# Transposed chunks laid out in runs of 384 columns, and the whole order of a fused recurrence and convolution laid anew

## The chip, the cores and the metric

The kernel runs on one core of a Trainium2 chip. The metric is the device time of one execution in microseconds (us). The compute engines of the core are PE (matrix products and transposes), DVE, ACT and POOL (elementwise work); SP issues the transfers, and 16 transfer engines carry them out. Each engine works through its own queue in order and waits on semaphores for the others.

## The reference

```python
def _attn_ref(r, k, v, w, u):          # B, H, S, D = 4, 8, 768, 48
    state = np.zeros((B, H, D, D))
    for t in range(S):
        cur = np.einsum('bhd,bhe->bhde', u[None] * kt, vt)
        y[:, :, t] = np.einsum('bhd,bhde->bhe', rt, state + cur)
        state = wt[:, :, :, None] * state + np.einsum('bhd,bhe->bhde', kt, vt)

def _moe_ref(x, w_proj, filter_fft, w_out):   # x: the y above as 4 x 768 x 384
    x1, x2, x3 = split(x @ w_proj, 3)
    x2_conv = irfft(rfft(x2, axis=1) * rfft(filter_fft, axis=0), axis=1)
    return ((x1 * x2_conv * x3) @ w_out).astype(np.float32)
```

A linear recurrence with a decay w and a bonus u gives y for 4 batches, 8 heads, 768 steps and 48 channels. Then y, as 768 x 384 for each batch, is projected three ways; the second projection is convolved along time with a filter, multiplied by the other two and projected out. Inputs and output are float32.

## The kernel before

Time is cut into chunks of 128 steps: 24 chunks, six to a batch (c is the chunk of all, ci its place in the batch). For each chunk the four slices of w, k, r and v are loaded (ldw, ldk, ldr, ldv: 192 KB each, into rings of six buffers). ACT takes the logarithm of w (lw); PE sums it along time by triangular masks (cs, ce) and ACT takes exponentials (en or enp, eq). These scale k and r (kh, q), which PE transposes (tqk) and ACT or DVE copies out of the bank (tT). sc is the product of the two within the chunk, mt its masked copy, kv and S the state that is handed on. rk, rku and cc make the bonus (r times k times u, summed over a head) and vc is v times it. y is summed in a bank; a step yb starts with a matmul that adds vc, a step y leaves it out, and DVE's xn adds it while it copies the bank (after yb, ACT's xc copies it). yt transposes y in three blocks of 128 channels, and xT copies that to SBUF.

In place of a transform of 768 points the kernel folds time. For the chunks 3 to 5 of a batch, sa and sb add and subtract the transposed chunk and its counterpart of the first half (into sd), fp and fm fold the sums once more (into fo), and x2 projects these by the second slice of w_proj. f transforms them by a matrix, da, db, ua and ub multiply by the filter's transform, pp adds, and i1 and i2 transform back. p1 and p3 are the other two projections: PE multiplies a slice of w_proj (stationary) by 384 columns of the transposed y (moving), three matmuls for each step. yy multiplies by their product g, po projects out, o copies the result and st stores it.

The three slices of w_proj and w_out are loaded by ldp0 to ldp3 (576 KB each, into o0), and ACT casts them (wc).

The order of all this is written out by hand in a string, ORDER (line 37), of 1094 words. Each word holds an engine (S, P, A, V and G for SP, PE, ACT, DVE and POOL), an operation with its chunk or its batch and part, and behind @ a bank. Line 864 emits word after word, so each engine's queue is the words of its letter in their order. Waits come from the buffers that the words share, and a word with ! also waits for DVE's last operation of a certain kind.

Before the change the transposed y of a batch lies as three rows (blocks of channels) of 768 columns, and a chunk is a piece of 128 columns in each:

```python
    xT_b = ring("xT", 2, [L, CB, S], BF16)       # L = 128, CB = 3, S = 768
    sd_b = ring("sd", 2, [L, CB, HALF], BF16)    # HALF = 384
```

Of the kernel before, what the change touches and what calls it, by code (L numbers as in the profile page):

```python
# [38 lines left out]
V:ang2 V:ang0 V:mem0 V:angn V:mem4 P:cs2@0 V:mem6 P:ce2@1 S:ldfilt A:en2 P:zs29@2 A:lw0 P:ce1@2
G:uc! G:mkd! V:mem5 V:fs S:ldk1 A:sin S:ldr1 S:ldk0 S:ldv0 S:ldr0 P:z7@0 P:zs2@0 P:ce0@3 P:hf0@0  # L40
P:cs1@4 V:rsc P:zs2@5 P:cs0@5 A:eq1 A:en1 A:eq0 A:ht0.1 A:v0 P:hf1@2 V:fd S:ldr3 P:hf2@4 P:hf3@3
A:enp0 A:ht0.0 V:rk1 V:q1 V:mem2 V:hr0.1 A:ht1.1 G:kh1! V:khp0 V:hr0.0 P:kv0@5 S:ldk3 V:hr1.1 G:q0!
A:eqp2 P:tqk0@0 V:S0 P:hf4@5 A:ht1.0 G:rk0! S:ldw3 V:rku1 P:tqk1@4 S:ldk2 S:ldr2 A:he P:hf5@2 G:rk3!
A:lw3 A:ph2 V:tT0 P:ce3@0 V:cc1 S:ldv1 V:rku0 A:ht2.1 S:ldw4 A:tT1 V:hr1.0 V:cc0 P:cs3@3 P:sc0@8
G:kh2! V:hr2.1 G:vc0! P:mtr1@4 V:qp2 P:tqk2@1 G:rk2! A:enp3 A:ht2.0 A:ms1 V:mt0 A:v1 S:ldw5 S:ldv2
P:kv1@5 A:tT2 V:rku3 V:rku2 V:hr2.0 P:sc1@8 P:mtr0@1 P:yb0@2 S:ldr4 S:ldk4 A:lw4 A:eq3 G:hb2! V:khp3
P:ce4@0 A:lw5 A:hb0 V:S1 P:cs5@3 A:xc0 P:cs4@5 V:ms0 V:cc2 G:q3! P:tqk3@2 V:mt1 A:eq4 V:cc3 P:mtr2@0
P:sc2@8 G:vc1! V:mt2 A:v2 A:en5 A:tT3 V:mc0 S:ldk5 P:kv2@3 G:rk4! G:vc2! A:ms2 A:enp4 P:yb1@2
P:sc3@8 G:q4! V:khp4 A:mc1 V:mt3 P:ce5@1 P:y2@4 S:ldw6 S:ldv3 A:v3 A:xc1 A:mc2 S:ldr5 V:S2 P:yt0@5
P:tqk4@2 P:kv3@0 G:kh5! A:eq5 P:yt1@1 G:vc3! S:ldw7 S:ldv5 A:lw6 V:rk5 V:rku4 V:rku5 A:lw7 V:S3  # L50
A:tT4 S:ldv4 S:ldr6 A:xT0 V:cc4 P:ce6@3 S:ldk6 G:q5! P:sc4@8 P:tqk5@2 V:xn2 G:v4! P:cs6@4 V:mt4
V:xT1 P:yb3@5 A:eq6 P:cs7@3 P:kv4@0 A:tT5 G:vc4! A:v5 A:en6 S:ldw8 S:ldp1 P:sc5@8 A:xc3 G:q6! V:cc5
P:yb4@2 P:yt3@5 P:yt2@4 G:rk6! A:lw8 A:xc4 P:ce7@1 V:S4 A:xT2 V:mt5 A:eq7 V:sa3 V:sb3 A:xT3 G:vc5!
# [842 lines left out]
```

## Time and profile before

| | |
|---|---|
| median of 3 runs | 158.87 us (158.29 to 159.4) |
| the profiled execution | 159.96 us, its span 158.3 us |
| busy PE, DVE, ACT, POOL | 136.4, 134.1, 131.2, 107.5 us |
| moved by DMA | 27.59 MB in 105,844 packets |
| mean granted clock of PE | 0.987 of full speed |

The span is the time from the first to the last instruction; the execution's own time is a little longer. Busy time is summed over an engine's instructions; matmuls overlap, so PE's is not its work at full pace. A transfer is issued by SP and lands some microseconds later; at most eight are under way, since each issue waits for the one eight places ahead of it.

### The profile page before, as it was taken

To read this page: it belongs to the slowest core of one execution; us is meant where nothing else is said; L and a number is where in the kernel's file an instruction comes from. 1 tells how busy PE (TensorE), PEld (TensorE's weight loads), DVE (VectorE), ACT (ScalarE), POOL (GpSimd) and SP (SyncE) were. 2 spreads that over 40 slices of the span, in tenths; PEclk is the share of its full clock that TensorE was granted. 3 is DMA by queue.
4 is the path that set the end of the run, shared out by engine and by line. 5 is a ranking of instruction groups with operands and counts; after the bars stand their busy time and mean duration, and the time that the engine had idled before them with its cause. 6 is when DMAs were issued, how large, how long until landed. Compare 5 with 4: busy or idle time off the path is not lost.

```text
span 158.3 us, 4054 instructions
## 1 busy us (share of the span) xinstructions
PE 136.4 (86%) x1492; PEld 89.0 (56%) x1492; DVE 134.1 (85%) x271; ACT 131.2 (83%) x274; POOL 107.5 (68%) x130
## 2 busy tenths in 40 slices
...
PEclk9999999999789999999999999999999999999998
DMA  5999989989898999979999979999940020000856
GB/s 105 189 297 178 205 162 211 209 171 255 178 234 207 205 195 196 214 149 222 203 177 261 222 148 221 190 206 246 247 159 0 4 99 4 0 2 35 326 205 233
DMA packets 105844, 27.59 MB, mean 174 GB/s; under 512 B 100320, under 2 KB 105824, under 8 KB 105824
## 3 DMA queue, kind: packets, MB, share of 16 engines
...
q8 instruction: 11, 0.18, 0.5%
...
## 4 chain that ended last, share of the span: by engine, by line
PE 40%; ACT 14%; DMA 13%; DVE 13%; SPq 9%; issue 4%; POOL 4%; ACTq 0%; POOLq 0%; DVEq 0%
SPq L452 9%; PE p L669 8%; PE x L700 7%; PE po L796 5%; DMA o<-in_moe_w_proj_dram 4%; DMA ldw<-in_w_dram 4%; DMA ldr<-in_r_dram 3%; ACT qkT L233 3%; PE f L720 3%; PE tqk L542 3%; DMA ldv<-in_v_dram 2%; PE sc L555 2%; PE i L754 2%; PE f L715 2%; DVE UA L742 2%
## 5 line engine op out<-in xcount | busy, mean ns | idle before, releaser
L669 PE MATMUL p<-xT,wproj 128*128 128x384 bf16 x144 | 29.6, 326 | 0.9 <-ACT qkT L233 0.9
L523 POOL TENSOR_TENSOR rk<-ldr,ldk 128x384 bf16<-128x384 f32 x21 | 21.3, 1018 | 6.2 <-DMA ldr<-in_r_dram 2.0
L562 DVE TENSOR_TENSOR mt<-sc,mask_excl 128x1024 bf16<-128x1024 f32 x21 | 25.5, 1213 | 0.0
L233 ACT ACTIVATE qkT<-tqk 128x1024 bf16<-128x1024 bf16 x21 | 21.8, 1039 | 0.7 <-PE tqk L542 0.7
L520 POOL TENSOR_TENSOR qk<-ldr,eq 128x384 bf16<-128x384 f32 x20 | 20.1, 1004 | 2.9 <-ACT eq L487 1.1
L536 POOL TENSOR_TENSOR vc<-v,cc 128x384 bf16<-128x384 bf16 x24 | 19.9, 832 | 2.8 <-ACT ab L233 1.3
L516 POOL TENSOR_TENSOR qk<-ldk,en 128x384 bf16<-128x384 f32 x12 | 12.0, 1000 | 12.8 <-ACT E L422 7.4
L669 PEld LDWEIGHTS <-wproj 128*128 128x128 bf16 x144 | 12.7, 97 | 8.8 <-issue 1.4
L542 PE MATMUL tqk<-ident,qk 128*128 128x128 bf16 x192 | 14.8, 219 | 2.3 <-DVE qk L510 1.1
L458 ACT ACTIVATE lg<-ldw 128x384 bf16<-128x384 f32 x24 | 12.8, 540 | 4.3 <-DMA ldw<-in_w_dram 4.3
L542 PEld LDWEIGHTS <-qk 128*128 128x128 bf16 x192 | 12.1, 98 | 5.6 <-issue 2.7
L796 PE MATMUL po<-wout,y 128*128 128x384 bf16 x72 | 14.3, 326 | 0.3 <-DVE y L788 0.3
L754 PE MATMUL i<-m_b,P 128*128 128x384 bf16 x72 | 14.0, 325 | 0.0
L233 ACT ACTIVATE x<-p 128x384 bf16<-128x384 f32 x24 | 11.9, 510 | 1.8 <-PE p L669 1.7
L233 ACT ACTIVATE ab<-x 128x384 bf16<-128x384 f32 x24 | 11.6, 509 | 1.8 <-PE x L700 1.6
L529 DVE TENSOR_REDUCE cc<-rku 128x8 f32<-128x384 bf16 x24 | 13.0, 540 | 0.0
L233 ACT ACTIVATE xT<-yt 128x384 bf16<-128x384 bf16 x20 | 10.1, 513 | 2.7 <-DVE sd L646 2.3
L462 PE MATMUL cs<-lg,mask_incl 128*128 128x384 bf16 x24 | 7.6, 331 | 5.5 <-ACT lg L458 5.1
L745 DVE TENSOR_TENSOR UB<-f,T 128x768 bf16<-128x768 f32 x11 | 10.3, 949 | 2.0 <-PE f L720 2.0
L487 ACT ACTIVATE eq<-ce 128x392 f32<-128x392 f32 (+1 forms) x23 | 11.6, 507 | 0.2
L591 DVE TENSOR_TENSOR S<-kv,eq 128x384 bf16<-128x384 f32 x20 | 10.9, 547 | 0.5 <-PE kv L583 0.5
L233 ACT ACTIVATE v<-ldv 128x384 bf16<-128x384 f32 x19 | 10.4, 545 | 1.2 <-DMA ldv<-in_v_dram 1.2
(143 smaller groups left out, 372.1 us busy)
## 6 DMA issues: line engine op xcount, KB each, us to landing
ldw<-in_w_dram SPq DMA_DIRECT2D x24, 192.0 KB, 3.9
ldk<-in_k_dram SPq DMA_DIRECT2D x24, 192.0 KB, 3.8
ldr<-in_r_dram SPq DMA_DIRECT2D x24, 192.0 KB, 4.0
ldv<-in_v_dram SPq DMA_DIRECT2D x24, 192.0 KB, 3.8
out_dram<-o SPq DMA_DIRECT2D x12, 192.0 KB, 2.5
out_dram<-filt SPq DMA_DIRECT2D x12, 192.0 KB, 2.1
o<-in_moe_w_proj_dram SPq DMA_DIRECT2D x3, 576.0 KB, 5.9
...
```

The costliest lines, as they stand in the source:

```text
L233: return nc.scalar.activation(out=o, in_=i, func=AF.Copy)
L452: nc.sync.dma_start(out=ld[x][c % LD], in_=src[b, :, ci * L:ci * L + L, :].rearrange("h t d -> t h d"),)
L458: nc.scalar.activation(out=lg_b[c % 3][:, :, 0:D], in_=ld["w"][c % LD], func=AF.Ln)
L520: return two(e).tensor_mul(qk_b[c % 3][:, 0, :, 0:D], ld["r"][c % LD], eq)
L523: return two(e).tensor_mul(rk_b[c % 2], ld["r"][c % LD], ld["k"][c % LD])
L529: nc.vector.tensor_reduce(out=cc_b[c % 3], in_=rku_b[c % 2], axis=AX.X, op=ALU.add)
L536: return two(e).tensor_mul(vc_b[c % 3], v_b[c % 4], cc_b[c % 3].to_broadcast([L, H, D]))
L542: nc.tensor.transpose(p[:, x, j, :], qk_b[c % 3][:, x, 2 * j:2 * j + 2, :], ident)
L562: nc.vector.tensor_mul(mt_b[c % 3], bank_of[f"sc{c}"].rearrange("p q j t -> p (q j) t"), dataclasses.replace(m[:, :], ap=[m[:, :].ap[0], [ ...
L669: nc.tensor.matmul(p, wproj[:, n, cb, fb * L:(fb + 1) * L], xT_b[b % 2][:, cb, sl], start=(cb == 0), stop=(cb == CB - 1),)
L754: nc.tensor.matmul(p, P_b[b % 2][:, s // 2, s % 2, cb * L:(cb + 1) * L], m_b[:, s].rearrange("p a t -> p (a t)"), start=(i == 0), stop=(i ...
L796: nc.tensor.matmul(p, y_b[0][:, cb, ti * L:(ti + 1) * L], wout[:, cb, :], start=(cb == FIRST[0]), stop=(cb == FIRST[-1]),)
```

## The change

Three things are changed. The tiles xT and sd are laid out chunk by chunk: the three blocks of a chunk follow each other, 384 columns in one run, and the chunks follow each other. What writes or reads one chunk (xT, sa, sb, fp, fm) now has one run where it had three of 128 (the sums of a batch's last chunk still write each block backwards). A projection, which reads three chunks of one block, had one run of 384 columns and now has three of 128, 384 columns apart. x2 with ti = 1 reads 128 columns in one run, as before.

Two operations are added, rh and ch, with a ring of buffers, another way to sum the bonus; no word of the order uses them.

The order is a new one of 1089 words. Nearly every word stands elsewhere, and some work goes to another engine or takes another form: 20 words move from DVE to POOL (five more rku there in the net) and 16 back; the bonus of chunks 14 to 17 is added by DVE (y and xn) where a matmul added it (yb), that of chunks 21 and 23 the other way round; one last copy of the result, o3.0, goes from ACT to DVE; two groups of warm-up matmuls at the start (z7, zs2) are gone.

```diff
--- before.py
+++ after.py
 ORDER = """
-S:ldw1 S:ldw2 G:iota! G:mki! G:iorot! S:ldw0 A:tLn A:lw2 V:mem3 V:mem1 G:mke! A:lw1 V:ang1 S:ldu
...
+S:ldw1 G:iota! G:mki! A:tLn G:iorot! S:ldk0 S:ldw0 V:ang1 V:ang0 V:mem0 V:ang2 A:lw1 G:mke! V:mem4
...
 """
@@ -164,6 +164,7 @@
     eq_b = ring("eq", 3, [L, C + 2 * HP], FP32)
     rk_b = ring("rk", 2, [L, H, D], BF16)
     rku_b = ring("rku", 2, [L, H, D], BF16)
+    rh_b = ring("rh", 2, [L, H, D // 2], FP32)
     v_b = ring("v", 4, [L, H, D], BF16)
     cc_b = ring("cc", 3, [L, H], FP32)
     vc_b = ring("vc", 3, [L, H, D], BF16)
@@ -171,8 +172,8 @@
     mt_b = ring("mt", 3, [L, H, L], BF16)
     S_b = ring("S", 3, [L, HP, 2, D], BF16)
     xn_b = ring("xn", 3, [L, C], BF16)
-    xT_b = ring("xT", 2, [L, CB, S], BF16)
-    sd_b = ring("sd", 2, [L, CB, HALF], BF16)
+    xT_b = ring("xT", 2, [L, NCH, CB, L], BF16)
+    sd_b = ring("sd", 2, [L, NT, CB, L], BF16)
     x1_b = ring("x1", 1, [L, CB, S], BF16)
     g_b = ring("g", 2, [L, CB, S], BF16)
     fo_b = ring("fo", 2, [L, 2, CB, L], BF16)
@@ -529,6 +530,13 @@
         nc.vector.tensor_reduce(out=cc_b[c % 3], in_=rku_b[c % 2], axis=AX.X, op=ALU.add)
 
 
+    def op_rh(e, c):
+        x = rku_b[c % 2]
+        return two(e).tensor_add(rh_b[c % 2], x[:, :, 0:D // 2], x[:, :, D // 2:])
+
+    def op_ch(e, c):
+        nc.vector.tensor_reduce(out=cc_b[c % 3], in_=rh_b[c % 2], axis=AX.X, op=ALU.add)
+
     def op_v(e, c):
         return copy(e, v_b[c % 4], ld["v"][c % LD])
 
@@ -632,9 +640,9 @@
 
     def sums(e, c, q):
         b, ci = bi(c)
-        lo = xT_b[b % 2][:, :, (ci - NT) * L:(ci - NT + 1) * L]
-        hi = xT_b[b % 2][:, :, ci * L:ci * L + L] if e == "G" else bank_of[f"yt{c}"]
-        o = sd_b[q][:, :, (ci - NT) * L:(ci - NT + 1) * L]
+        lo = xT_b[b % 2][:, ci - NT]
+        hi = xT_b[b % 2][:, ci] if e == "G" else bank_of[f"yt{c}"]
+        o = sd_b[q][:, ci - NT]
         if ci == NCH - 1:
             o = dataclasses.replace(
                 o, offset=o.offset + (L - 1) * o.ap[-1][0],
@@ -650,35 +658,35 @@
 
     def op_fp(e, b, q):
         return two(e).tensor_add(
-            fo_b[q][:, 0], sd_b[q][:, :, 0:L], sd_b[q][:, :, 2 * L:3 * L],
+            fo_b[q][:, 0], sd_b[q][:, 0], sd_b[q][:, 2],
         )
 
     def op_fm(e, b, q):
         return two(e).tensor_sub(
-            fo_b[q][:, 1], sd_b[q][:, :, 0:L], sd_b[q][:, :, 2 * L:3 * L],
+            fo_b[q][:, 1], sd_b[q][:, 0], sd_b[q][:, 2],
         )
 
     def op_xT(e, c):
         b, ci = bi(c)
-        copy(e, xT_b[b % 2][:, :, ci * L:(ci + 1) * L], bank_of[f"yt{c}"])
-
-
-    def proj(name, bank, b, n, fb, sl):
+        copy(e, xT_b[b % 2][:, ci], bank_of[f"yt{c}"])
+
+
+    def proj(name, bank, b, n, fb, hf):
         p = ps(name, bank)
         for cb in range(CB):
             nc.tensor.matmul(
-                p, wproj[:, n, cb, fb * L:(fb + 1) * L], xT_b[b % 2][:, cb, sl],
+                p, wproj[:, n, cb, fb * L:(fb + 1) * L], xT_b[b % 2][:, NT * hf:NT * hf + NT, cb, :],
                 start=(cb == 0), stop=(cb == CB - 1),
             )
 
     def op_p1(e, b, fb, hf, bank):
-        proj(f"p1.{b}.{fb}.{hf}", bank, b, 0, fb, halves[hf])
+        proj(f"p1.{b}.{fb}.{hf}", bank, b, 0, fb, hf)
 
     def op_x1(e, b, fb, hf):
         copy(e, x1_b[0][:, fb, halves[hf]], bank_of[f"p1.{b}.{fb}.{hf}"])
 
     def op_p3(e, b, fb, hf, bank):
-        proj(f"p3.{b}.{fb}.{hf}", bank, b, 2, fb, halves[hf])
+        proj(f"p3.{b}.{fb}.{hf}", bank, b, 2, fb, hf)
 
     def op_g(e, b, fb, hf):
         sl = halves[hf]
@@ -698,7 +706,7 @@
         p = ps(f"x2.{b}.{q}.{ti}", bank)
         for cb in range(CB):
             nc.tensor.matmul(
-                p, sd_b[q][:, cb, L:2 * L] if ti == 1 else fo_b[q][:, ti // 2, cb, :],
+                p, sd_b[q][:, 1, cb, :] if ti == 1 else fo_b[q][:, ti // 2, cb, :],
                 wproj[:, 1, cb, :],
                 start=(cb == 0), stop=(cb == CB - 1),
             )
```

Three places show how the order moves. First SP's queue around the load of w_out. A name's number is that of the ring's buffer, chunk modulo six: ldr4 in these rows is chunk 16, ldr5 is chunk 17, ldw0 chunk 18, ldk3 chunk 15. Both pieces begin at the 66th transfer. Before:

```order
L452 DMA ldv1_98<-in_v_dram 128x8x48
L452 DMA ldk3_88<-in_k_dram 128x8x48
L452 DMA ldw4_83<-in_w_dram 128x8x48
L452 DMA ldr4_95<-in_r_dram 128x8x48
L452 DMA ldv2_99<-in_v_dram 128x8x48
L452 DMA ldw5_84<-in_w_dram 128x8x48
L452 DMA ldk4_89<-in_k_dram 128x8x48
L452 DMA ldv3_100<-in_v_dram 128x8x48
L355 DMA o0_167<-in_moe_w_out_dram 128x3x384
L452 DMA ldv4_101<-in_v_dram 128x8x48
L452 DMA ldk5_90<-in_k_dram 128x8x48
L452 DMA ldr5_96<-in_r_dram 128x8x48
```

In the changed kernel:

```order
L453 DMA ldv1_98<-in_v_dram 128x8x48
L356 DMA o0_169<-in_moe_w_out_dram 128x3x384
L453 DMA ldk3_88<-in_k_dram 128x8x48
L453 DMA ldr3_94<-in_r_dram 128x8x48
L453 DMA ldk4_89<-in_k_dram 128x8x48
L453 DMA ldv2_99<-in_v_dram 128x8x48
L453 DMA ldr4_95<-in_r_dram 128x8x48
L453 DMA ldv3_100<-in_v_dram 128x8x48
L453 DMA ldk5_90<-in_k_dram 128x8x48
L453 DMA ldv4_101<-in_v_dram 128x8x48
L453 DMA ldr5_96<-in_r_dram 128x8x48
L453 DMA ldw5_84<-in_w_dram 128x8x48
```

The load of w_out went from the 74th place to the 67th, ahead of the loads k15, r15, k16, v14, r16 and v15, and w17 (ldw5) from the 71st to the 77th.

Second, DVE's queue at the sums of batch 2 (sd0 are the sums sa, sd1 the differences sb; yt15 to yt17 the banks of chunks 15 to 17). Before, chunk 17's pair stands behind the reduction cc, two pairs SD, khp (qk) and S:

```order
L646 TENSOR_TENSOR sd0_143<-xT0_141,yt16_1995 128x3x128
L649 TENSOR_TENSOR sd1_144<-xT0_141,yt16_1995 128x3x128
L529 TENSOR_REDUCE cc0_123<-rku0_117 128x8
L785 TENSOR_TENSOR SD0_160<-i1_1_0_2000,E0_157 128x2x192
L776 TENSOR_TENSOR SD0_160<-i1_1_0_2000,E0_157 128x2x192
L504 TENSOR_TENSOR qk1_107<-cs19_1966,ldk1_86 128x8x48
L785 TENSOR_TENSOR SD2_162<-i1_1_2_2025,E2_159 128x2x192
L591 TENSOR_TENSOR S0_135<-kv18_2046,eq0_112 128x384
L646 TENSOR_TENSOR sd0_143<-xT0_141,yt17_2054 128x3x128
L649 TENSOR_TENSOR sd1_144<-xT0_141,yt17_2054 128x3x128
```

The same place of DVE's queue in the changed kernel:

```order
L657 TENSOR_TENSOR sd1_146<-xT0_143,yt16_1881 128x384
L570 TENSOR_TENSOR mt2_136<-sc17_1918,mask_excl_180 128x1024
L654 TENSOR_TENSOR sd0_145<-xT0_143,yt16_1881 128x384
L628 TENSOR_TENSOR xn0_140<-y15_1938,vc0_128 128x384
L505 TENSOR_TENSOR qk1_107<-cs19_1936,ldk1_86 128x8x48
L628 TENSOR_TENSOR xn2_142<-y17_1981,vc2_130 128x384
L784 TENSOR_TENSOR SD2_164<-i1_1_2_1975,E2_161 128x2x192
L657 TENSOR_TENSOR sd1_146<-xT0_143,yt15_1994 128x384
L654 TENSOR_TENSOR sd0_145<-xT0_143,yt15_1994 128x384
```

Chunk 16 now comes ahead of chunk 15, its copies xn are DVE's, and of chunk 17 only the difference is left on DVE (four rows further on); its sum, sa17, is POOL's.

Third, the end of ACT's queue, the last copies of the result (o2 and o3 by the banks po; before, then changed):

```order
L233 ACTIVATE o0_167<-po_2_2_2724 128x384
L233 ACTIVATE filt_166<-po_3_3_2759 128x384
L233 ACTIVATE filt_166<-po_3_1_2762 128x384
L233 ACTIVATE filt_166<-po_3_5_2773 128x384
L233 ACTIVATE filt_166<-po_3_2_2754 128x384
L233 ACTIVATE filt_166<-po_3_4_2788 128x384
L233 ACTIVATE filt_166<-po_3_0_2778 128x384
```

The end of ACT's queue in the changed kernel:

```order
L234 ACTIVATE o0_169<-po_2_2_2717 128x384
L234 ACTIVATE o0_169<-po_2_0_2713 128x384
L234 ACTIVATE filt_168<-po_3_3_2756 128x384
L234 ACTIVATE filt_168<-po_3_1_2747 128x384
L234 ACTIVATE filt_168<-po_3_5_2762 128x384
L234 ACTIVATE filt_168<-po_3_4_2750 128x384
L234 ACTIVATE filt_168<-po_3_2_2768 128x384
```

po_3_0 is gone from ACT's end and is the last row of DVE's queue.

More of the change, by code (lines that the diff above doesn't have):

```diff
@@ L37 @@
 ORDER = """
-S:ldw1 S:ldw2 G:iota! G:mki! G:iorot! S:ldw0 A:tLn A:lw2 V:mem3 V:mem1 G:mke! A:lw1 V:ang1 S:ldu
[L39 to L53, printed above, removed]
@@ L95 @@
-V:cc17 A:xc16 P:ce20@5 A:eq20 G:kh20! P:yt15@0 P:i21.2@4 P:p32.0.0@3 G:vc17! G:rk20! G:q20! S:ldk23
-S:ldr23 V:sa15 V:sb15 P:cs19@2 A:v18 A:ec1.2 A:x12.2.0 V:g2.0.0 V:mt17 P:i21.0@5 P:i21.1@4 P:tqk18@1
-A:enp19 S:st0.3 A:ec1.0 A:xT15 A:ec1.1 P:yt16@3 V:sa16 P:i11.0@5 A:tT18 A:xT16 P:yb17@0 P:x22.0.1@4
-G:gm1.2.1! P:i11.2@1 A:xc17 V:sb16 V:cc18 V:d1.0 G:vc18! G:q19! G:rk19! A:ab2.0.1 P:tqk20@3 P:kv18@0
-V:s1.0 V:khp19 V:d1.2 P:yt17@5 S:ldv22 V:S18 A:lw22 V:sa17 A:xT17 V:sb17 P:p32.2.0@4 P:sc18@8
```

160 lines of the change are left out of this document (90 added, 70 removed).

## The prediction

> **What bounds the kernel now.** I read the page first, for the balance of the engines.
>
> ```profile
> PE 136.4 (86%) x1492; PEld 89.0 (56%) x1492; DVE 134.1 (85%) x271; ACT 131.2 (83%) x274; POOL 107.5 (68%) x130
> PEclk9999999999789999999999999999999999999998
> DMA  5999989989898999979999979999940020000856
> ```
>
> No engine stands out by its share, so the share says little. The last row says more: the transfer engines are full from slice 1 to slice 28 (about 115 us) and nearly idle after it. The PEclk row has one dip, in slices 10 and 11.
>
> The windows of 4 us (in each: length, busy time and count of PE, PEld, DVE, ACT, POOL, then clock, DMA share and rate) show which stage is full where.
>
> ```profile
> 20.00:24.00 4.00, 2.52 (x38) 1.78 (x37) 3.46 (x8) 3.50 (x7) 2.88 (x4) 1.00 0.83 159
> 40.00:44.00 4.00, 2.84 (x16) 1.52 (x17) 3.70 (x10) 2.89 (x6) 2.12 (x3) 0.67 0.85 191
> 44.00:48.00 4.00, 4.00 (x33) 1.98 (x31) 1.59 (x3) 3.85 (x8) 2.76 (x4) 0.90 0.94 210
> 68.00:72.00 4.00, 2.92 (x46) 1.92 (x44) 4.00 (x8) 2.80 (x8) 2.53 (x4) 1.00 0.75 151
> 104.00:108.00 4.00, 3.27 (x40) 2.02 (x39) 3.40 (x8) 1.72 (x5) 3.07 (x4) 1.00 1.12 220
> 108.00:112.00 4.00, 3.09 (x24) 1.64 (x22) 3.14 (x9) 3.98 (x7) 2.02 (x3) 1.00 1.03 247
> 120.00:124.00 4.00, 4.00 (x48) 2.66 (x46) 4.00 (x9) 3.80 (x8) 3.67 (x5) 1.00 0.02 4
> ```
>
> From 112 us on PE is never idle, so the end is the moment at which PE has done its list. The chain of waits (start, length, what) shows from where that list runs without a large hole.
>
> ```profile
> 34.63 5.85 DMA o<-in_moe_w_proj_dram
> 40.50 1.17 ACT wproj L233
> 41.72 4.08 PE x L700 x15
> 64.99 5.57 DMA ldw<-in_w_dram
> 98.25 0.33 PE cs L462 x2
> 152.61 0.94 ACT filt L233 x3
> ```
>
> The second slice of w_proj (ldp1) lands at 40.5, ACT casts it, and the first x2 starts at 41.72. Everything after that is PE's list plus its holes, and then the last copies and stores. The waits of PE inside 41.7 to 153.7 (engine, line, awaited: us in total, times, longest) are the holes that the profile shows:
>
> ```profile
> PE x L700 <- ACT wproj L233: 1.2, 1, 1.2
> PE ce L468 <- ACT xn L233: 1.1, 1, 1.1
> PE p L669 <- ACT qkT L233: 0.9, 1, 0.9
> PE yt L631 <- DVE SD L776: 0.6, 1, 0.6
> PE po L796 <- DVE y L788: 0.3, 1, 0.3
> PE x L700 <- ACT qkT L233: 0.2, 1, 0.2
> ```
>
> The 1.2 is the wait for w_proj itself. Two of the others are of interest. The 1.1 ends at 71.5: ACT had sat behind the w load that was issued at 64.99 and took 5.57 to land. The 0.6 and the 0.9 fall in 104 to 110, where ACT is busy for only 1.72 of 4 us. A further loss is no wait: fifteen x2 matmuls take 4.08 us, where two matmuls of the same 384 columns take 0.33 at 98.25, so fifteen should take 15 x 0.163 = 2.45; the slow clock of that place (0.67) costs 1.63.
>
> The last matmuls of the PE queue (start, length, count) end at 153.65:
>
> ```profile
> 151.85 1.80 PE L796 MATMUL po<-wout,y 128*128 128x384 bf16 x10 [0.27 <-DVE y L788]
> ```
>
> So the account of the profiled execution is: 41.7 up to the first x2, 112 of PE with about 3.1 of visible holes and 1.6 of slow clock in it, and 4.6 behind the last matmul: 158.3 of span. The execution's own time is 159.96; the three plain runs have a median of 158.87, so 1.1 of it belongs to that execution. I make the sum as a difference in the span and apply it to 158.87.
>
> **The layout.** It changes addresses, not instructions: the same 24 copies, 12 pairs of sums, 8 pairs of folds and 144 projection matmuls. The rows by form (busy, mean ns) of what it touches, beside a neighbour with other addresses:
>
> ```profile
> L669 PE MATMUL p<-xT,wproj 128*128 128x384 bf16 x144 | 29.6, 326 | 0.9 <-ACT qkT L233 0.9
> L233 ACT ACTIVATE ab<-x 128x384 bf16<-128x384 f32 x24 | 11.6, 509 | 1.8 <-PE x L700 1.6
> L233 ACT ACTIVATE xT<-yt 128x384 bf16<-128x384 bf16 x20 | 10.1, 513 | 2.7 <-DVE sd L646 2.3
> L468 PE MATMUL ce<-lg,mask_excl 128*128 128x384 bf16 x24 | 8.0, 341 | 1.2 <-ACT xn L233 1.1
> L462 PE MATMUL cs<-lg,mask_incl 128*128 128x384 bf16 x24 | 7.6, 331 | 5.5 <-ACT lg L458 5.1
> L646 DVE TENSOR_TENSOR sd<-xT,yt 128x384 bf16<-128x384 bf16 x11 | 3.7, 344 | 0.0
> L652 DVE TENSOR_TENSOR fo<-sd 128x384 bf16<-128x384 bf16 x5 | 1.8, 361 | 0.0
> ```
>
> The copy that writes three runs (513 ns) costs what the copy into one run costs (509), so the writers gain nothing that can be seen: at most 24 x 4 ns, 0.1 us. The reader gets worse addresses: the projection's moving operand was one run of 384 columns and is now three runs of 128. The nearest rows are cs and ce, whose moving operand (lg) comes in eight runs of 48: 331 and 341 against 326. That bounds the cost between 0 and 144 x 15 ns = 2.2 us; two cs follow each other at 0.33, the full pace, so I take 0. The Trainium skill speaks against the change if it is read widely: "Advanced Engine Details and Errata", Memory Cachelines, says that any non-contiguous access pattern slows matmuls significantly. It says so of PSUM, which the projection still writes in one run, and the rows of lg show no such price for the moving side.
>
> **The order.** PE first. Behind the first x2 the new list has one cs less (cs8's place), and two y steps that begin without the bonus matmul of 384 columns (four yb of batch 2 become y, two y of batch 3 become yb); DVE adds the bonus there instead. Three matmuls of 0.163 are 0.49 us. **-0.5.** The start up to 41.72 I take as unchanged: ldp1 is the 32nd transfer in both lists and the 31 ahead of it are the same set. The bounds are 0.7 us either way: that is what the queue left idle in its worst window there (0.83 of 4 us, 20 to 24). The dropped warm-up matmuls lie before it, where PE waits anyway.
>
> The end: six copies of the last po (filt) stand behind the last matmul on ACT, and now the one of po.3.0 goes to DVE, which is done by then. By the chain, three of them take 0.94, the span of two steps and a tail, so one is 0.3 to 0.5. **-0.4**, and nothing below that.
>
> The place at 104 to 110. The page's waits there (engine, line, awaited: total, times, longest):
>
> ```profile
> ACT xT L233 <- DVE sd L646: 2.3, 1, 2.3
> DVE sd L649 <- ACT xT L233: 1.9, 2, 1.3
> ```
>
> Chunk 17's copy on ACT (xT17) waited for DVE's sum of the same bank, sa17, which stands behind cc, d, s, khp, d and S on DVE; ACT's queue behind xT17 (tT20, lw21, tT19) waited with it, and PE's 0.6 and 0.9 are what that left. The new list hands these banks over fewer times: xT16 and xT17 come ahead of their sums, and sa17 is on POOL, which reads the copy in SBUF. Only xT15 still waits for sums. Gain: 1.5 at most; what the same queues then wait for the trace cannot show, and a new hole could eat it all. I take half: **-0.75**.
>
> The hole at 70.4 to 71.5, 1.1 long, is a late load (the median of such loads is 3.9, below). In the new list that load, w14, is 59th instead of 58th, and PE has 191 steps of its list behind the first use of it (cs14 or ce14), not 200. Between 0 and -1.1; half again: **-0.55**.
>
> One move goes the other way. SP's issues around the load of w_out (start, length):
>
> ```profile
> 78.40 1.65 SPq L452 DMA_DIRECT2D ldw<-in_w_dram  x1
> 80.15 0.78 SPq L452 DMA_DIRECT2D ldk<-in_k_dram  x1
> 81.64 1.13 SPq L355 DMA_DIRECT2D o<-in_moe_w_out_dram  x1
> 83.98 2.56 SPq L452 DMA_DIRECT2D ldr<-in_r_dram  x1
> ```
>
> ```profile
> ldw<-in_w_dram SPq DMA_DIRECT2D x24, 192.0 KB, 3.9
> o<-in_moe_w_proj_dram SPq DMA_DIRECT2D x3, 576.0 KB, 5.9
> ```
>
> ldp3 moves from the 74th to the 67th place, so k15, r15, k16, v14, r16 and v15 are queued behind 576 KB where they were ahead of it. A transfer of that size lands 2.0 later (5.9 against 3.9), and the issue that had to wait behind it took 2.56. In the old list that was r17; in the new one it is about r16, for which PE has 13 steps between the issue and tqk16 in the list, where it had 30. Between 0 and +2.0; the 13 steps, at 0.33 to 0.49 each, cover a landing of 3.9 and POOL's q16 but little more: **+0.6**. As w_out is cast by ACT only when it is there, no store or po waits for it sooner.
>
> What DVE, ACT and POOL have to do hardly changes (DVE 264 to 261 rows, ACT 274 to 272, POOL 133 to 135), and POOL, which gains five rku, is idle for a third of the span. The last loads are far ahead of their use (r23's issue on SP, and tqk23 on PE):
>
> ```profile
> 110.38 0.71 SPq L452 DMA_DIRECT2D ldr<-in_r_dram  x1
> 124.47 0.61 PE L542 MATMUL tqk<-ident,qk 128*128 128x128 bf16 x8
> ```
>
> With 14 us between the two, what moves among the loads of chunks 18 to 23, and the two early stores that now follow the last loads, costs nothing.
>
> Sum: -0.5 - 0.4 - 0.75 - 0.55 + 0.6 = -1.6, so 158.9 - 1.6 = **157.3 us**.
>
> **The rivals.** *The clock.* The dip at 40 to 48 came when PE took up fifteen matmuls at once after a wait of 1.2. The new list breaks the row: twelve of x2, then sc6, then three. If the clock stays at 1.00, 1.63 more is gained: 155.7. For it: no other wait of about 1 us is followed by a dip (68 to 72 has 1.00). Against it: the wait for ldp1 stays. The Trainium skill ("TensorE: Matmul & The Clock Gate", Part 1) says that the clock falls to half after an idle window of some 3.4 us; by that rule a wait of 1.2 leaves the clock alone, and the dip would be an accident that need not come back. The 0.67 in the row after a wait of 1.2 speaks against reading it so.
>
> *The holes close.* If both holes go whole (2.6) and ldp3 costs nothing: -0.5 - 0.4 - 2.6 = -3.5, 155.4.
>
> *Like for like.* The new list has new holes of the same size: only -0.9 is left, 158.0.
>
> *Slower: ldp3 starves chunks 15 and 16.* The loads behind it are issued 2.56 late and land in 5.57, as the w load of 64.99 did, not 3.9: 4.2 us on the way to tqk16. Without the +0.6 the sum was -2.2, so the end is at +2.0, 160.9. It decides from a hole of 2.2 us before tqk16 on, and makes the kernel slower by 1% from 3.8 on. For it: up to there the loads are used as they land. Against it: ring slots are free then, and PE has po and f of batch 1 to run.
>
> *Slower: the layout.* 2.2 on the projections gives 159.5, still within 1%; only twice that, which no row here shows, makes it slower, 161.7.
>
> **How the numbers follow.** 1% of 158.87 is 1.6 us, about what can be told from no change: 157.3 to 160.5. Forecast 0.40 (156.5 to 159.0, of it 0.12 under 157.3), clock 0.14, holes close 0.14, like for like 0.10, ldp3 0.18, layout 0.04. Faster: 0.12 + 0.14 + 0.14 = 0.40; the same: 0.28 + 0.10 = 0.38; slower: 0.18 + 0.04 = 0.22. The range of 155.0 to 160.7 holds the cases at 155.4 and 155.7 and leaves out half of the slower ones and what lies beyond two gains at once.
>
> **What would show it.** The first x2 should start between 40.3 and 43. PE's waits behind it should lack the one for ACT xn at 70 and those of 104 to 110, ACT's wait for DVE sd should be under 1, and no single wait of PE before tqk16 over 1. The last copies should be five on ACT and one on DVE. Projection matmuls should still read 326 ns. It would be wrong if x2 started some us earlier or later, since everything behind it moves along, if PEclk shows another dip, or if PE waits for POOL's q or for a load in chunks 14 to 17.

## The result and the profile after

The changed kernel takes 159.74 us (median of 20 runs), the kernel before in the same runs 158.81. The ratio is 1.0061, with an interval of 1.0035 to 1.0088: slower by 0.6%, where 157.3 and a gain of 1% had been forecast. The first profile of the changed kernel fell into a disturbed execution (granted clock 0.84), so the rows below are of the same kernel profiled again (the first run of the next section), with a span of 158.7 us against 158.3 before. From its page, the balance of the engines, the clock and the transfer engines:

```profile
PE 134.9 (85%) x1480; PEld 88.7 (56%) x1480; DVE 134.1 (85%) x269; ACT 130.3 (82%) x272; POOL 107.6 (68%) x132
...
PEclk9995699999999999999999999999999999999999
DMA  5799999999899989989999999999601080001855
```

PE's busy time fell by 1.5 us. The dip of the clock at 40 to 48 us is gone, and there is one at 12 to 20 us, ahead of the first x2. Nothing in these rows says why the kernel is not faster. The waits of PE behind the first x2 do (engine, line, awaited: us in total, times, longest):

```profile
PE y L611 <- DVE sd L654: 1.5, 1, 1.5
PE x L708 <- ACT wproj L234: 1.3, 1, 1.3
PE p L677 <- ACT xT L234: 1.3, 2, 0.7
PE i L762 <- DVE SD L793: 0.7, 1, 0.7
PE yt L639 <- DVE sd L654: 0.5, 1, 0.5
PE p L677 <- DVE sd L654: 0.4, 1, 0.4
```

Four of the six rows are about one kind of bank, that of the transposed chunk (yt): ACT's copy xT reads it, DVE's sums sa and sb (sd) read it, and PE waits for the copy, or for the bank to come free. In the kernel before, the one place of this kind that showed, at 104 to 110, cost PE 0.6 and 0.9. (The row of i, at 61 us, is no such handover, and three of seven profiles of the new order lack it.) Where the holes lie shows in five windows from 44 to 144 us (length, busy time and count of PE, PEld, DVE, ACT, POOL, clock, DMA share, rate); first the changed kernel:

```profile
44.00:68.00 24.00, 23.11 (x267) 15.19 (x265) 22.47 (x37) 22.91 (x48) 20.43 (x24) 1.00 1.00 205
68.00:80.00 12.00, 9.94 (x109) 6.53 (x106) 9.01 (x23) 9.69 (x24) 6.89 (x8) 1.00 0.95 205
80.00:100.00 20.00, 20.00 (x246) 13.41 (x243) 20.00 (x34) 19.29 (x43) 16.78 (x20) 1.00 1.02 199
100.00:112.00 12.00, 9.99 (x111) 6.72 (x110) 9.72 (x24) 9.57 (x22) 8.21 (x9) 1.00 0.97 201
112.00:144.00 32.00, 31.82 (x334) 20.58 (x333) 31.30 (x58) 25.94 (x58) 24.54 (x25) 1.00 0.17 56
```

The same windows of the order before, from the run that keeps it and changes the layout alone:

```profile
44.00:68.00 24.00, 23.70 (x278) 15.12 (x276) 23.23 (x39) 23.26 (x50) 20.98 (x23) 1.00 1.02 210
68.00:80.00 12.00, 11.68 (x126) 7.88 (x123) 12.00 (x29) 11.49 (x28) 7.99 (x10) 1.00 0.92 180
80.00:100.00 20.00, 19.57 (x253) 13.35 (x252) 19.77 (x35) 18.70 (x41) 15.80 (x20) 1.00 1.03 214
100.00:112.00 12.00, 10.31 (x109) 6.51 (x106) 9.79 (x24) 9.70 (x21) 8.04 (x9) 1.00 0.98 209
112.00:144.00 32.00, 32.00 (x325) 20.64 (x323) 30.56 (x56) 26.08 (x59) 25.49 (x25) 1.00 0.16 50
```

PE is idle 2.06 us from 68 to 80 where it was idle 0.32, and 2.01 from 100 to 112 where it was idle 1.69. Seven profiles of the new order with its handovers as they are, this one among them, have 9.94 to 9.96 and 9.97 to 9.99 there: this is no scatter. The order before, in its four profiles (in two of them with one word moved), has 10.7 to 11.8 at 68 to 80.

The two ends of PE's list in the changed kernel (start, length, line, what, count, and the idle time ahead of it) stand against 41.72 and 151.85 before:

```profile
40.57 1.14 PE L708 MATMUL x<-wproj,sd 128*128 128x384 bf16 x6 [1.32 <-ACT wproj L234]
...
151.56 1.80 PE L804 MATMUL po<-wout,y 128*128 128x384 bf16 x10 [0.34 <-DVE y L796]
```

Behind them come the last six stores, by SP's rows of the changed kernel:

```profile
152.45 3.34 SPq L824 DMA_DIRECT2D out_dram<-filt  x6
```

They begin 0.29 earlier than before (152.74), and the span ends 0.4 later.

The rest of the account, profile against profile (span 157.1 of the run with the layout alone, 158.7 of the changed kernel): the first x2 starts at 40.57 instead of 42.12, a gain of 1.55; from there to the last y on DVE it takes 110.4 instead of 108.0, a loss of 2.4; from the last y to the end 7.7 instead of 7.0, a loss of 0.7. The sum is +1.6, where the plain runs show about a microsecond. A single profile is good to some tenths: two more of the order before, each with one word moved (further down), start x2 at 41.8 and 41.4 and have 108.3 and 108.4 for the middle part, so the loss there lies between 2.0 and 2.4. (The kernel before in its own profile has 109.5, with the late load and the slow clock that the prediction tells of.) It is all idle time: from the first x2 to the last y PE is busy for 105.15 us in the changed kernel and for 105.22 with the layout alone.

### The profile page after: what moved, and what is told of

The parts are those of the page before. It is cut to its first block, busy times and chain, and to the rows that moved or that the text cites. A ratio compares the mean times of both kernels' runs of the same rounds, so it can differ in the third digit from the quotient of the medians.

```text
span 167.4 us, 4030 instructions
## 1 busy us (share of the span) xinstructions
PE 145.7 (87%) x1480; PEld 93.2 (56%) x1480; DVE 135.7 (81%) x269; ACT 131.8 (79%) x272; POOL 107.9 (64%) x132
## 4 chain that ended last, share of the span: by engine, by line
PE 65%; ACT 15%; DVE 8%; DMA 6%; issue 2%; SPq 1%; ACTq 0%; DVEq 0%
PE p L677 15%; PE x L708 8%; PE po L804 7%; PE i L762 7%; PE tqk L550 5%; PE f L728 4%; DMA o<-in_moe_w_proj_dram 3%; PE sc L563 3%; DMA ldw<-in_w_dram 3%; ACT qkT L234 2%; PE f L723 2%; DVE mt L570 2%; PE kv L591 2%; PE ce L469 2%; PE y L616 2%
## 5 line engine op out<-in xcount | busy, mean ns | idle before, releaser
L677 PE MATMUL p<-xT,wproj 128*128 128x384 bf16 x144 | 32.8, 353 | 1.5 <-ACT xT L234 1.0
L521 POOL TENSOR_TENSOR qk<-ldr,eq 128x384 bf16<-128x384 f32 x22 | 22.0, 1002 | 9.5 <-DVE qk L294 4.2
L234 ACT ACTIVATE qkT<-tqk 128x1024 bf16<-128x1024 bf16 x23 | 23.6, 1028 | 1.1 <-PE tqk L550 0.9
L550 PE MATMUL tqk<-ident,qk 128*128 128x128 bf16 x192 | 16.0, 231 | 0.5 <-DVE S L599 0.5
L804 PE MATMUL po<-wout,y 128*128 128x384 bf16 x72 | 15.9, 356 | 0.3 <-DVE y L796 0.3
L762 PE MATMUL i<-m_b,P 128*128 128x384 bf16 x72 | 15.7, 355 | 0.0
L550 PEld LDWEIGHTS <-qk 128*128 128x128 bf16 x192 | 13.3, 102 | 3.3 <-issue 0.7
L527 POOL TENSOR_TENSOR rku<-rk,u_bc 128x384 bf16<-128x384 bf16 x13 | 11.8, 914 | 0.7 <-DVE y L796 0.6
L708 PE MATMUL x<-wproj,fo 128*128 128x384 bf16 x48 | 10.9, 358 | 0.0
L693 DVE TENSOR_TENSOR g<-p,x 128x384 bf16<-128x384 f32 x17 | 9.2, 552 | 1.8 <-PE p L677 1.8
```

What stands on the lines that cost most here:

```text
L234: return nc.scalar.activation(out=o, in_=i, func=AF.Copy)
L521: return two(e).tensor_mul(qk_b[c % 3][:, 0, :, 0:D], ld["r"][c % LD], eq)
L550: nc.tensor.transpose(p[:, x, j, :], qk_b[c % 3][:, x, 2 * j:2 * j + 2, :], ident)
L677: nc.tensor.matmul(p, wproj[:, n, cb, fb * L:(fb + 1) * L], xT_b[b % 2][:, NT * hf:NT * hf + NT, cb, :], start=(cb == 0), stop=(cb == CB - 1),
L708: nc.tensor.matmul(p, sd_b[q][:, 1, cb, :] if ti == 1 else fo_b[q][:, ti // 2, cb, :], wproj[:, 1, cb, :], start=(cb == 0), stop=(cb == CB ...
L762: nc.tensor.matmul(p, P_b[b % 2][:, s // 2, s % 2, cb * L:(cb + 1) * L], m_b[:, s].rearrange("p a t -> p (a t)"), start=(i == 0), stop=(i ...
```

## The experiments

A ratio is to the kernel before, run on the same chip, with its interval. The groups of runs below were made on different chips, so ratios of one group compare more surely than those of two.

**The changed kernel again, the layout alone, the order alone.** The second run takes ORDER as it was and the two tiles in the new layout; the third the reverse.

```diff
-    xT_b = ring("xT", 2, [L, CB, S], BF16)
-    sd_b = ring("sd", 2, [L, CB, HALF], BF16)
+    xT_b = ring("xT", 2, [L, NCH, CB, L], BF16)
+    sd_b = ring("sd", 2, [L, NT, CB, L], BF16)
```

> The changed kernel once more, for an undisturbed profile beside the kernel before on one chip. By its 20 runs it should come out at 1.004 to 1.009 of the kernel before. Theory A (the new order moved the handovers of the yt banks between ACT's copies and DVE's sums instead of removing them): the profile shows PE holes of 1 us or more in sum at 69 to 80 and at 104 to 112, while everything before 41 us is as predicted. Theory B (the dropped warm-up matmuls let the clock fall early): the granted clock is under 0.9 somewhere between 8 and 24 us and the first x2 starts later than 42.5. Theory C (ldp3's earlier place starves chunks 15 and 16): one wait of PE over 1 us just ahead of tqk16 or tqk17.

> The kernel before, its order word for word, with the tiles xT and sd laid out chunk by chunk as in the change. The prediction put the layout at 0, with bounds of 0 and +2.2 us. If it costs nothing: 158.6 to 159.0 (ratio 0.998 to 1.002), and the projection matmuls read 326 ns again. If the three runs of 128 columns cost the reader what the matmuls of lg cost (331 to 341 ns): up to +2.2 us, ratio up to 1.014. If the whole loss of the change (+0.9) is the layout's, the ratio is 1.006.

> The kernel before, its layout of thirds kept, with the order of the changed kernel word for word. If the loss is the order's alone: ratio 1.004 to 1.009 as in the changed kernel. If the layout costs and the order gains (as the prediction had it, -1.6): ratio 0.99. If the layout gained by its shorter address lists and the order lost more: a ratio over 1.01.

Changed kernel 1.0089 (1.0051 to 1.0127), layout alone 1.0005 (0.9967 to 1.0044), order alone 1.0070 (1.0030 to 1.0111). The layout costs nothing that these runs can tell: the projections read 326 ns, to the nanosecond what they read before, in this row by form (busy, mean ns) of the run with the layout alone:

```profile
L669 PE MATMUL p<-xT,wproj 128*128 128x384 bf16 x144 | 29.6, 326 | 1.1 <-ACT qkT L233 0.9 <-ACT xT L233 0.2
```

The whole loss is the order's. Of the three theories for it, C falls (PE is busy for 20.00 of 20 us from 80 to 100, where the loads behind w_out are used), and so does B: the clock does fall to 0.50, but the first x2 comes earlier, not later. A stays: its holes are there, 2.06 and 2.01 of idle PE in the two windows.

**The handovers at chunks 9 and 10.** The holes at 68 to 80 come like this. ACT's copy xT9 stood ahead of the sums of chunk 9, xT10 behind those of chunk 10. In the changed kernel DVE waited 1.44 for xT9, then did qk and mt, and only then the sums of chunk 10, for which ACT's xT10 waited 2.28. PE's yt waited for the bank, and its p for the copy (start, length, line, instruction, idle time ahead of it):

```profile
69.32 0.35 DVE L657 TENSOR_TENSOR sd<-xT,yt 128x384 bf16<-128x384 bf16 x1 [1.44 <-ACT xT L234]
70.00 0.33 PE L639 MATMUL yt<-ident,xn 128*128 128x128 bf16 x3 [0.47 <-DVE sd L654]
72.16 0.49 ACT L234 ACTIVATE xT<-yt 128x384 bf16<-128x384 bf16 x1 [2.28 <-DVE sd L657]
72.70 0.65 PE L677 MATMUL p<-xT,wproj 128*128 128x384 bf16 x3 [0.73 <-ACT xT L234]
```

In the order before, DVE made the copy of chunk 10 itself (V:xT10), so there was nothing to hand over there; the new order gave that word to ACT. The edit turns both pairs round:

```diff
-A:xT9 ... V:sb9 V:sa9 ... V:sa10 ... V:sb10 V:g1.1.0 A:xT10
+V:sb9 V:sa9 A:xT9 ... A:xT10 V:sa10 V:sb10 V:g1.1.0
```

> The changed kernel with three words moved at chunks 9 and 10: DVE's sums of chunk 9 ahead of ACT's copy xT9 of the same bank, and the copy xT10 ahead of the sums of chunk 10. In the changed kernel PE lost 0.47, 0.15 and 0.73 us at 69.5 to 72.7 because the two engines read those banks in the other order (ACT waited 2.28 for DVE, DVE 1.44 for ACT). Theory (the handovers were moved, not removed, and they are what the new order lost): these three holes go and the kernel gains 1.0 to 1.3 us, ratio to the kernel before 0.998 to 1.002. Rival (the loads set the pace up to 113 us, so a hole closed at 70 opens again later): gain under 0.3, ratio 1.005 to 1.009, and a new hole between 75 and 105.

158.45 us, ratio 0.9960 (0.9916 to 1.0004), 1.3% below the ratio of the changed kernel above. The windows 68 to 80 and 100 to 112 of this kernel:

```profile
68.00:80.00 12.00, 11.66 (x141) 8.14 (x139) 11.16 (x26) 11.95 (x29) 8.78 (x10) 1.00 0.98 211
100.00:112.00 12.00, 9.98 (x99) 6.58 (x98) 10.76 (x26) 9.59 (x20) 6.94 (x9) 1.00 1.02 210
```

1.72 us of PE's time are back in the first, and nothing is lost again in the second. From the first x2 to the last y it takes 108.8 instead of 110.4. The rival (the loads set the pace up to 113) falls.

**The handover at chunk 16.** In the changed kernel DVE's rows around 102 us (start, length, line, instruction, and the idle time ahead of it) show the other hole from DVE's side:

```profile
100.03 0.54 DVE L530 TENSOR_REDUCE cc<-rku 128x8 f32<-128x384 bf16 x1
102.37 0.35 DVE L657 TENSOR_TENSOR sd<-xT,yt 128x384 bf16<-128x384 bf16 x1 [1.81 <-ACT xT L234]
102.64 1.22 DVE L570 TENSOR_TENSOR mt<-sc,mask_excl 128x1024 bf16<-128x1024 f32 x1
103.78 0.34 DVE L654 TENSOR_TENSOR sd<-xT,yt 128x384 bf16<-128x384 bf16 x1
```

DVE has nothing to do for 1.81 us until ACT has copied the bank, does one of the two sums, then mt17, then the other sum; the bank comes free at about 104.1. PE's y17 wants that bank:

```profile
104.17 0.33 PE L611 MATMUL y<-S,qkT 128*128 128x96 bf16 x4 [1.49 <-DVE sd L654]
```

The edit puts both sums ahead of the copy, into DVE's idle time:

```diff
-A:xT16 V:cc17 V:sb16 P:tqk18@5 A:ec1.2 V:mt17 G:vc17! V:sa16
+V:cc17 V:sb16 V:sa16 A:xT16 P:tqk18@5 A:ec1.2 V:mt17 G:vc17!
```

> The changed kernel with DVE's two sums of chunk 16 put ahead of ACT's copy xT16 and ahead of mt17 on DVE. In the changed kernel DVE sat idle for 1.81 us until xT16 had read the bank, did one sum, then mt17 (1.22), then the other sum, and PE's y17 waited 1.49 for that bank. Theory: the hole of 1.49 at 102.7 and that of 0.52 at 107 shrink to under 0.6 together and the kernel gains 1.0 to 1.5 us, ratio 0.997 to 1.002. Rival (loads set the pace): under 0.3, ratio 1.005 to 1.009, with PE waiting somewhere else before 116.

158.55 us, ratio 1.0034 (0.9976 to 1.0093). The ratio lies above what was expected, and its interval overlaps the theory's range and holds the rival's, so it decides nothing; the profile does. From the first x2 to the last y it takes 108.7 instead of 110.4. The hole of 1.49 is gone, the sums run at 100.76 and 101.02, and the window 100 to 112 has 11.52 of 12 (the other window contains a dip of the clock here, to 0.86):

```profile
68.00:80.00 12.00, 10.51 (x93) 6.78 (x92) 8.72 (x23) 8.95 (x21) 5.83 (x8) 0.86 0.94 201
100.00:112.00 12.00, 11.52 (x125) 7.71 (x122) 11.52 (x28) 11.40 (x24) 8.68 (x10) 1.00 1.03 210
```

**The end, and the three edits together.** poa.3.2 was put ahead of the last y, the last pob nearly in a row, and the copies of them on ACT and DVE in turn (SP's words and d3.1 are left out here):

```diff
-V:yy3.1 P:pob3.3 P:poa3.5@1 A:o3.3 P:pob3.1 P:poa3.2@5 P:pob3.0 P:pob3.5 V:o3.0 A:o3.1 P:pob3.2 A:o3.5 P:pob3.4 ... A:o3.4 A:o3.2
+P:poa3.2@5 V:yy3.1 P:pob3.3 P:pob3.1 A:o3.3 P:pob3.0 V:o3.1 P:pob3.2 A:o3.0 P:poa3.5@1 V:o3.2 P:pob3.4 A:o3.4 P:pob3.5 ... V:o3.5
```

> The changed kernel with another end: poa.3.2 ahead of the last y, the six last pob nearly in a row, three of the last copies on ACT and three on DVE in turn, and the last stores issued in the order in which the copies end. In the changed kernel the last y starts 0.29 earlier than before but the span ends 0.4 later: from the last y to the end 7.75 us against 7.06. Theory (the end was mis-sized: the copies were not the bound, the order of matmuls and stores behind the last y is): 6.9 us or less from the last y to the end, a gain of 0.7 to 1.0, ratio 0.999 to 1.004. Rival (the transfer engines' rate alone sets the end): gain under 0.2.

> The three edits together. If they are independent: 2.7 to 3.8 us less than the changed kernel, 156.2 to 157.2 against 159.0 before, ratio 0.983 to 0.991, which is where the prediction put the change. If the loads set the pace up to 113 us: only the parts behind it count, 1.5 to 2.0 us, ratio 0.995 to 0.998.

The end alone gave nothing: 1.0084 (1.0051 to 1.0117), a miss, and from the last y to the end it is still 7.5 us. All three together take 156.11 us, ratio 0.9807 (0.9754 to 0.9860), about 2% faster than the kernel before. In their profile it takes 107.1 from the first x2 to the last y, 3.3 less than in the changed kernel, which is what the two handovers gave one by one (1.5 and 1.7). The two without the end were not run together; since the end gave nothing, the gain is put down to them. That the plain time fell by more than the single runs add up to (3.7 below the run of the end on the same chip, where they give 1.4 and 1.3) is not explained.

**The copy o3.0, and the place at 104 to 110 in the kernel before.** What the end lacked showed in the transfers. From the issue of the first of the last six stores to the end of the span it takes 5.5 us in the kernel before and 6.2 in the changed one. Rows of the transfer engines from 150 to 160 us, in 40 slices of 0.25 us (busy tenths, then GB/s); the kernel before:

```profile
DMA  9881059997000059999999999992000000000000
GB/s 363 344 344 51 0 211 344 344 375 289 25 18 0 0 221 387 363 363 363 369 357 375 369 369 350 375 381 80 0 0 0 0 0 0 0 0 0 0 0 0
```

The changed kernel:

```profile
DMA  1000899930000999950599999998000000000000
GB/s 39 0 0 6 332 375 381 369 111 0 0 0 0 297 338 344 375 185 25 215 393 369 381 350 381 363 369 332 31 6 0 0 0 0 0 0 0 0 0 0
...
q1 hardware_dynamic: 1159, 1.57, 42.6%
q14 instruction: 2, 0.02, 0.8%
```

At full pace the 16 engines move about 370, so one of them about 23. The tails of 25 and 18 and of 31 and 6 fit one engine that is alone at work, late behind the others. The span ends 1.3 us behind the last packet of a store in both kernels, so such a tail at the very end counts in full. The queue q14 carries instructions: 8 KB each, in a single packet, so on one engine. In the kernel before the last of them runs at 151.3, and its tail (25 and 18) is over before the last six stores move data; in the changed kernel it runs at 153.4, among them. Two runs asked whether the moved copy causes this, a third mended the handovers and put all last copies on ACT. The edit of the first:

```diff
-V:o3.0 A:o3.1 P:pob3.2 A:o3.5 P:pob3.4 S:st3.1 S:st3.0 A:o3.4 A:o3.2 S:st3.4 S:st3.2 S:st3.5
+A:o3.1 P:pob3.2 A:o3.5 P:pob3.4 S:st3.1 S:st3.5 A:o3.2 A:o3.4 A:o3.0 S:st3.4 S:st3.0 S:st3.2
```

> The changed kernel with one word back: the last copy o3.0 on ACT again, and the last six stores in the order that the kernel before has. The prediction put this copy's move to DVE at -0.4, so undoing it should cost 0.4 (ratio to the kernel before 1.010). Theory now: the move lost time. In every profile of the new order one packet of 8 KB of instructions is fetched while the last six stores stream out (153.4 in the changed kernel), one of the 16 transfer engines ends 0.5 to 0.75 us after the others, and from the first of these stores to the end it takes 6.0 to 6.25 us, against 5.5 in the kernel before, where the fetch comes ahead of the stores (151.3). If DVE's late instruction is what triggers the fetch, with o3.0 on ACT it comes ahead of the stores again and the stretch is 5.5 to 5.7: a gain of 0.3 to 0.6, ratio 1.003 to 1.005. If the fetch belongs to another engine, it stays at about 153 and the stretch at 6.0 or more.

> The kernel before with only o3.0 moved from ACT to DVE. Prediction's term: -0.4, ratio 0.9975. Theory of the late fetch: the copies end 0.4 sooner but a fetch of 8 KB of instructions falls among the last stores and takes that back or more; from the first of the last six stores to the end 5.9 to 6.2 instead of 5.5, ratio 1.000 to 1.003.

> The changed kernel with the handovers at chunks 9, 10 and 16 mended as in the runs of those, and the end with the matmuls nearly in a row, but all six last copies on ACT. Theory of the late fetch: against the run with three copies on DVE (156.1 us) the copies end 0.6 later, and the stores end 0.5 sooner behind them, so 155.6 to 156.3, ratio 0.978 to 0.983; the stretch from the first of the last six stores to the end is 5.5 to 5.7. If the fetch is not DVE's: that stretch stays at 6.0 or more and the time is 156.3 to 156.8.

With the copy back on ACT the changed kernel has 1.0138 (1.0097 to 1.0179), no gain, and a span of 158.7 as in the changed kernel's profile; the fetch stays at 153.5 and the stretch at 6.1. In the kernel before with the copy on DVE the ratio is 1.0031 (0.9987 to 1.0075), the fetch stays ahead of the stores and the stretch at 5.51; the copy on DVE brings nothing. So DVE's late instruction is not the cause. The third has 155.52 us and 0.9798 (0.9754 to 0.9842).

The fourth run of this group took the place at 104 to 110 in the kernel before by itself:

```diff
-V:S18 A:lw22 V:sa17 A:xT17 V:sb17
+A:xT17 V:S18 A:lw22 V:sa17 V:sb17
```

> The kernel before with one word moved: ACT's copy xT17 ahead of DVE's sum sa17 of the same bank (and ahead of lw22 on ACT). In the kernel before ACT waits 2.3 us there and PE loses 0.9 and part of 0.6 us behind it at 104 to 110. The prediction took half of that place, -0.75, as what a mended handover gives. If that price was right: a gain of 0.5 to 1.0, ratio 0.994 to 0.997, with the hole of 0.9 gone. If the hole only moves (DVE then waits for xT17, or the loads set the pace): within 0.3, ratio 0.998 to 1.002.

158.11 us, ratio 0.9971 (0.9935 to 1.0007). PE's window 100 to 112 goes from 10.31 (above) to 11.17:

```profile
100.00:112.00 12.00, 11.17 (x114) 7.04 (x112) 10.57 (x26) 10.57 (x23) 8.57 (x10) 1.00 1.00 210
```

The 0.9 hole is closed. That the kernel gained by it is not shown: the interval of the ratio holds 1, and from the first x2 to the last y its profile has 108.4, beside 108.0 and 108.3 in the two others of the order before.

**Whose fetch it is.** SP's, ACT's and DVE's queues are each some instructions longer or shorter in the new order. Four tiny loads on SP, six tiny copies on ACT and six on DVE, each in a kernel of its own, move that engine's place in its instructions and no other's. One such run was made with each on the changed kernel, and two on the version with mended handovers:

```diff
 S:st0.2
+S:pad0 S:pad1 S:pad2 S:pad3
```

> The changed kernel with four tiny loads of 2 KB added to SP's queue at about 112 us, where SP has nothing to issue and the transfer engines are idle; their data is used by nothing. The fetch that falls among the last stores comes in every profile when SP has run about 177 of its instructions (175 to 177 in the kernel before, 176 to 182 in those with the new order), and SP's queue of the new order is three instructions shorter (194, not 197). Theory (the fetch is SP's own, and slid into the tail because SP's queue is shorter): with four loads more it comes at 149.5 to 152, ahead of the last six stores, the stretch from the first of them to the end falls from 6.0-6.25 to 5.5, and the kernel gains 0.5, ratio to the kernel before 1.002 to 1.005. Rival (it belongs to another engine, or one engine of 16 is late for another reason): the fetch stays where it was, 0.9 behind the first of these stores, and the stretch stays at 6.0 or more.

> The run with the handovers at chunks 9, 10 and 16 mended and another end, all last copies on ACT, with the same four tiny loads. If the late fetch is SP's: the stretch falls from 5.92 to 5.5 and the time from 155.5 to about 155.1, ratio 0.975 to 0.980. If not: 155.5, ratio 0.978 to 0.983.

> The version with mended handovers and the other end once more, beside the one with four tiny loads, on one chip: 155.5, ratio to the kernel before 0.978 to 0.983, and 0.3 to 0.5 us slower than its companion if the late fetch is SP's, the same if not.

```diff
 A:X3.3
+A:pad0 A:pad1 A:pad2 A:pad3 A:pad4 A:pad5
```

> The changed kernel with six tiny copies (4 columns each, into a tile that nothing reads) added to ACT's queue at about 141 us, where ACT waits 2.2 us for PE. SP's four extra loads left the late fetch where it was, so it is not SP's. In every profile ACT had run 318 to 324 of its instructions when the fetch came, and its queue of the new order is four instructions shorter (327, not 331). Theory (the fetch is ACT's): with six more it comes at 149 to 152, ahead of the last stores, the stretch from the first of the last six stores to the end falls to 5.5 and the kernel gains 0.5 us, ratio 1.002 to 1.005. Rival (not ACT's): the fetch stays 0.9 to 1.4 behind the first of these stores, stretch 6.0 or more.

> The changed kernel with the same six tiny copies, but on DVE, at about 145 us. Theory (the fetch is DVE's, which has 330 instructions in the new order and 324 before): the fetch moves ahead by a microsecond or more and the stretch falls to 5.5. Rival (ACT's, or another engine's): fetch and stretch stay, 0.9 to 1.4 behind the first store and 6.0 or more, and the six copies cost 0.0 to 0.6.

> The version with mended handovers at chunks 9, 10 and 16 and the other end, all last copies on ACT, with the six tiny copies on ACT. If the fetch is ACT's: the stretch is 5.5 and the ratio to the kernel before 0.975 to 0.979; if not, 0.978 to 0.983 as without them.

SP's loads moved nothing: fetch at 153.8, stretch 6.25, ratio 1.0021 (0.9984 to 1.0058; the plain time lies lower than the profile, for which there is no reason at hand). DVE's copies moved nothing there either (155.2 behind a last y at 152.7) and cost more than expected, 1.0182 (1.0125 to 1.0239): they stand ahead of a g on which PE then waits 1.3 us. Another fetch did move with them, from 0.85 ahead of the last y to 2.3 ahead of it. ACT's copies did it: the late fetch, 2.5 behind the last y in the changed kernel, now comes at 148.9, 1.9 ahead of it, while the one at 149.9 keeps its place. The transfer rows of this run from 150 to 160 have no gap and no tail any more:

```profile
DMA  0007999500005999999999999200000000000000
GB/s 25 6 0 270 350 381 369 203 0 0 0 0 209 369 350 369 387 338 369 381 381 326 387 375 387 92 0 0 0 0 0 0 0 0 0 0 0 0 0 0
```

The stretch is 5.50, and from the last y to the end 6.99 instead of 7.73, with six instructions more on ACT and no other word moved. The fetch is ACT's. Over all profiles the stretch is 5.50 or 5.51 in the six in which no fetch falls among the last stores, and 5.91 to 6.25 in the thirteen in which one does. The plain times don't settle it: the ratio is 1.0009 (0.9973 to 1.0045), hardly below the 1.0021 of SP's loads, where nothing moved, and both are from other chips than the 1.0061 and 1.0089.

On the version with mended handovers the six copies give 155.64 us, 0.9805 (0.9749 to 0.9862), beside 0.9807 (0.9759 to 0.9856) without them and 0.9796 (0.9752 to 0.9839) with SP's loads. Its profile has the stretch of 5.51, where the other two have 5.95 and 6.00; the plain times don't tell these three apart, and the spans (154.0, 154.6 and 154.0) don't either. All three are about 2% faster than the kernel before.

## Why the prediction was wrong, step by step

The step that failed is the reading of the order at the handovers: it counted two holes as gains (-0.75 and -0.55), where the new order has larger ones at the same two places (+0.3 and +1.7). The end, which was to gain 0.4, lost 0.7. That the time still came within 1% of the kernel before is luck: an early start that was not counted offsets a good part of the loss behind it.

- **The start** (taken as unchanged, 0.7 either way). The first x2 comes at 40.1 to 41.2 in fourteen of fifteen profiles of the new order (41.7 in the other), at 41.4 to 42.1 in the four of the order before: a gain of about 1.0 that was not counted. The load of the second slice of w_proj is issued at 33.88 in the changed kernel, at 34.63 in the kernel before; what else gives the gain was not tried.
- **The layout** (0, up to +2.2). Right: 326 ns, ratio 1.0005. The Trainium skill ("Advanced Engine Details and Errata", Memory Cachelines) says of PSUM that non-contiguous patterns slow matmuls; for a moving operand in SBUF, in three runs of 128 columns, these runs show no such price.
- **PE's work** (-0.5). Not borne out: the three matmuls are gone, but from the first x2 to the last y PE is busy for 105.15 us, where the order before has 105.2 to 105.4 in three profiles. At most 0.25 of it can be seen. No run has this term alone.
- **The place at 104 to 110** (-0.75). This step failed. "The new list hands these banks over fewer times" was read from chunk 17 alone, and a copy that comes ahead of its sums was counted as a handover gone, where DVE then waits for the copy (1.81 at chunk 16). The hole moved to chunk 16, as copy, sum, mt, sum: 2.01 idle instead of 1.69. What mending chunk 17 alone is worth in the kernel before stays open: the window got 0.86 of PE's time back, and no gain of the whole is shown. Mending chunk 16 in the changed kernel took 1.7 off the way from the first x2 to the last y.
- **The hole at 70** (-0.55). This failed most, on two counts. The late load belonged to one execution: three other profiles of the same order have 11.4 to 11.8 of 12 us busy there, against 10.74, so there was little to gain. And the prediction did not look at what the new order does there with the banks of chunks 9 and 10, which costs PE 1.74 more. It is the same pattern as at 104, one batch earlier, and stood in the same list.
- **ldp3** (+0.6) costs nothing: PE is busy throughout from 80 to 100. The rival of 160.9 falls with it.
- **The end** (-0.4, "and nothing below that"). It was mis-sized and has the other sign: +0.7. The six stores, not the copies, are what ends last; a copy less on ACT is worth 0.0 (7.02 from the last y to the end in the kernel before, with the copy on ACT and with it on DVE), and ACT's instruction fetch among the stores costs 0.7.
- **The rivals.** *Like for like* named the mechanism, new holes for old, but took them as equal in size; they were 2.1 larger at the two places, and the end turned. *Holes close* had 155.4, and the mended versions take 155.5 to 156.4, but by edits that the change does not have. *The clock*: the dip at 40 to 48 is gone, as that rival had it, and the kernel is slower all the same. It is no gain of the change, since the order before also shows the dip elsewhere (35 to 39 with the layout alone) or, with o3.0 on DVE, not at all. The rule of the Trainium skill ("TensorE: Matmul & The Clock Gate", Part 1), half clock after an idle window of some 3.4 us, is near what the changed kernel shows, where 0.50 follows four microseconds (8 to 12) with PE busy for 0.85. It does not explain the 0.67 at 40 to 44 before, after a wait of 1.2, nor 0.51 at 72 to 75.5 in the run with chunk 16 mended, behind four microseconds with PE busy for 2.55. Nor was it the row of fifteen matmuls that brought the dip of the kernel before: the clock is at 0.50 from 41.4 on, and the first x2 starts at 41.72.

Why the sums wait at all, though the copy and they only read: the Trainium skill ("PSUM — Partial Sum Buffer", "PSUM bank collisions raise a hardware error") says that the compiler's scheduler orders any two instructions of different engines on the same bank and the same 32 partitions, reads too. The trace agrees that such reads are ordered: ACT's read waited 2.28 for DVE's reads of the same bank, and DVE's 1.81 for ACT's.
